# Turning the whole q, k and alpha tensors on 64x64 tiles of TensorE instead of full ones

## The chip, the cores and the metric

The kernel runs on one core of a Trainium2 chip. The metric is the device time of one execution in microseconds. The engines are called as the profile calls them: PE is TensorE (PEld its weight loads), DVE is VectorE, ACT is ScalarE, POOL is GpSimd, and SP issues DMAs.

## What is computed

A gated linear attention and behind it a gated state space block. The sizes are B = 4, H = 8, S = 768, D = 48; the second block has a model width of 384 (H times D) and 512 inner channels.

```python
for t in range(S):                                   # attention, for each of 4 x 8 heads
    state = alpha[t][:, None] * state + outer(k[t], v[t])      # 48 x 48
    y[t] = q[t] @ state
x = y, heads side by side                            # (B, S, 384)
val, gate = split(x @ w_in)                          # 512 each
h[t] = exp(A_log) * h[t-1] + val[t]                  # along the sequence
out = (silu(gate) * h) @ w_out                       # (B, S, 384)
```

## The kernel before, in words

The sequence of each batch is cut into blocks of 256 steps; there are 12 blocks, m = 0 to 11, three per batch. The function `fast` does all the work for inputs in a usual range; the function `general` is a slow way for others and does not run here. The weights come as double precision numbers and are put together from their halves by bit operations (`low` on ACT, `high` on DVE, `add_low` on POOL).

For one block the attention goes in these stages:

- q, k and alpha are loaded with the time steps along the partitions. They have to be turned, so that head and channel lie along the partitions and time along the free axis. For blocks 4 and later, and for some tensors of block 3, DVE does that (`turn`, L600). In the first blocks PE does it, by a matmul with the identity matrix or by its transpose, and ACT copies the result from PSUM to SBUF (`copy_turned`, L713 and L714).
- DVE scans alpha into running products P (`scan_P`, L635) and backwards into V (`scan_V`, L654), and multiplies: Zk = k times V (`scaled_k`, L619), Zq = q times P (`scaled_q`, L610). In blocks 0 and 2 this is done for the two chunks of 128 steps one by one.
- `scores` (PE, L798) multiplies Zq and Zk for chunk 0 and then chunk 1, `masks` (DVE L808, ACT L810) takes the lower triangle, `values`, `states` and `carried` (PE, L834, L866, L847) make the output y and the running state, `add_banks` (DVE, L894) sums the states, and `join` (L960, L963) puts the heads in their places by copies and DMAs.

The second block of the kernel follows one attention block behind: `project(n, cc)` (L988) multiplies by a quarter of `w_in`, DVE scans the value part along the sequence (L995), ACT takes the silu of the gate (L1006), and `output` or `output_parts` (L1022, L1064) multiplies by `w_out`.

Everything stands in an order written out by hand (`manual_schedule`): each engine runs its instructions in the order of the Python calls. The order at L1119 to L1228 is what matters here. The banks of PSUM that the turned tensors use are taken from a fixed list of four tags (`taken`, L682), also written by hand: a call of `bank()` takes the next one, and `bank_pair()` the next two. A bank is free again when all that read it have done so.

A raw tile of q, k or alpha holds 128 partitions by 2 times 384 values. Partition c has the steps 8c to 8c + 7 of the block, so j, from 0 to 7, is the step within a partition; i, 0 or 1, is the half of the heads. To turn a whole tensor, `turn_over` (L764) takes the j in two halves of four, each in a bank of its own, and copies each half when it is turned. `turned` (L697) has two ways. For (0, k), (1, alpha), (1, k), (1, q) and (3, alpha) it issues, for each j, one transpose of 128 columns (L702) and one of 64 columns (L703) into the same bank. For the others it issues, for each j, two matmuls (L707), one for each i, with 64 columns of the raw tile as weights and the 128 columns of the identity moving.

`turn_over` is called six times: `straighten(0, "k")` at L1124, `alphas(1)` at L1125, `alphas(2)` at L1198, `straighten(2, "k")` at L1205, `straighten(2, "q")` at L1207 and `alphas(3)` at L1220. The tensors of block 1 that are turned half by half (L1131, L1139, L1149, L1163) call `turned` directly. The very first tensors have functions of their own; `first_alphas` (L716) turns alpha of block 0 on four tiles of 64x64, with the two halves of the rows in two banks.

Of the kernel before, what the change touches and what calls it, by code (L numbers as in the profile page):

```python
# [13 lines left out]
AF = mybir.ActivationFunctionType  # L14
# [332 lines left out]
def fast(  # L347
# [22 lines left out]
    nc = tc.nc  # L370
    B, H, S, D = q.shape
# [24 lines left out]
    NJ = GC // 32  # L396
    ROW = NJ * D
# [18 lines left out]
    def steps_of(name, m):  # L416
        return raws[name][:, ds(m % 2 * (2 * ROW + 16), 2 * ROW + 16)]
# [50 lines left out]
    ident = const.tile([C, C], FP32, name="ident")  # L468
# [127 lines left out]
    def by_runs(t):  # L596
        return t.rearrange("p h (c j) -> p h c j", j=NJ)
# [89 lines left out]
    def bank(tag=None):  # L687
        if tag:
            return ps_at.tile([C, 512], FP32, tag=tag, name=tag)
        return ps_mm.tile([C, 512], FP32, tag=f"mm{next(taken)}", name="mm")  # L690

    def bank_pair(tag=None):
        return [bank(tag and f"{tag}{i}") for i in range(2)]
# [3 lines left out]
    def turned(m, name, js, t, by_transpose=None):  # L697
        raw = steps_of(name, m)
        tp = t[:, 0:len(js) * C].rearrange("p (j x) -> p j x", j=len(js))
        if (m, name) in turned_by_transpose if by_transpose is None else by_transpose:  # L700
            for n, j in enumerate(js):
                nc.tensor.transpose(tp[:, n], raw[:, ds(ROW + j * D - 64, C)], ident)  # L702
                nc.tensor.transpose(tp[0:64, n], raw[:, ds(j * D, 64)], ident)  # L703
            return tp.rearrange("p j (c h) -> p h c j", h=4)
        for n, j in enumerate(js):
            for i in range(2):
                nc.tensor.matmul(tp[ds(64 * i, 64), n], raw[:, ds(i * ROW + j * D, 64)], ident,  # L707
                                 start=True, stop=True, skip_group_check=True)
        return tp.rearrange("p j (c h) -> p h c j", h=4)

    halves = [range(0, NJ // 2), range(NJ // 2, NJ)]

    def copy_turned(to, js, tp):  # L713
        nc.scalar.activation(by_runs(to)[:, :, :, js.start:js.stop], tp, AF.Copy)  # L714
# [47 lines left out]
        return to  # L762

    def turn_over(m, name, to):  # L764
        for js in halves:
            copy_turned(to, js, turned(m, name, js, bank()))

    def alphas(m):
        turn_over(m, "a", by_place(als[m % 2])[:, :, 1:GP])

    def straighten(m, name):
        to = plain(name)
        turn_over(m, name, to)
        return to
# [171 lines left out]
    for h in range(H):  # L946
        i, e, s = h // 4, h % 4 // 2, h % 2 ^ h // 4
# [183 lines left out]
    part = turned(1, "k", halves[0], bank())  # L1131
# [7 lines left out]
    part = turned(1, "k", halves[1], bank())  # L1139
# [9 lines left out]
    part = turned(1, "q", halves[0], bank())  # L1149
# [13 lines left out]
    part = turned(1, "q", halves[1], bank(), False)  # L1163
# [27 lines left out]
    for n in range(N):  # L1191
        m = n + 1
# [223 lines left out]
```

## Time and profile before

| | |
|---|---|
| median of 3 runs | 270.44 us (270.08 to 271.02) |
| the profiled execution | 269.92 us |
| its span | 268.2 us |
| instructions in the profile | 9966 |
| TensorE clock granted | 1.0 |
| DMA | 41.19 MB in 52304 packets |

The profile's page gives for each engine the busy time and its share of the span. Its fourth part is the chain of work that ended last: from the last instruction back to what released it, step by step. The trace behind the page can be asked for single stretches: a timeline lists the instructions of an engine in order, with start, length, engine, line, operation, output and input; equal neighbours are merged, with their count behind an x, and the length then goes from the first start to the last end. An fp32 matmul stands in the trace as two records, each with a weight load, and a transpose as one. A matmul's own length holds the time through the array, so the steps from start to start tell the pace, not the lengths.

### The profile page before, as it was taken

Reading aid. Unit: us, or ns where it says so; the run is one execution under the profiler, and the core shown is the slowest. Engines: PE = TensorE matmul, PEld = TensorE weight load, DVE = VectorE, ACT = ScalarE, POOL = GpSimd, SP = SyncE. Lnnn points to the kernel's source line nnn. Section 1 sums busy time; section 2 is a strip of 40 time slices with the busy share of each in tenths; the row PEclk is TensorE's granted clock in tenths of the full one; section 3 lists DMA queues with packets and bytes.
Section 4 is the critical chain, followed back from the end, with each engine's and each line's share of the span. In section 5 each row is a group of like instructions: output and inputs, shape, how many; then the busy total and the mean of one; then the engine's idle time right before and its main releaser. Section 6 shows DMA issues by size and latency. Waiting matters only on the chain.

```text
span 268.2 us, 9966 instructions
## 1 busy us (share of the span) xinstructions
PE 263.3 (98%) x4168; PEld 230.4 (86%) x4168; DVE 233.8 (87%) x316; ACT 111.6 (42%) x270; POOL 165.9 (62%) x185
## 2 busy tenths in 40 slices
PE   8999999999999999999999999999999999999995
PEld 6898889876688988988988988988988989988874
DVE  7979998996999999799999998999999998883440
ACT  4667766372342542532533533524524515214011
POOL 8222313084169997689985995996876986646000
PEclk9999999999999999999999999999999999999999
DMA  5947984998784569496487488569598501201101
GB/s 177 315 147 242 286 192 154 238 201 194 218 204 112 127 172 218 117 230 155 108 227 167 105 215 182 124 169 212 127 214 170 143 2 31 77 0 39 69 7 59
DMA packets 52304, 41.19 MB, mean 154 GB/s; under 512 B 27392, under 2 KB 50944, under 8 KB 52256
## 3 DMA queue, kind: packets, MB, share of 16 engines
q1 hardware_dynamic: 49328, 37.34, 56.2%
q0 software_dynamic: 1536, 2.20, 3.1%
q10 hardware_dynamic: 1392, 0.99, 1.3%
q8 instruction: 34, 0.56, 0.9%
q14 instruction: 14, 0.11, 0.1%
HBM read 32.54 MB, written 4.72 MB: 139 GB/s over the span
## 4 chain that ended last, share of the span: by engine, by line
PE 91%; DVE 2%; DMA 2%; issue 1%; ACT 1%; POOL 1%; SPq 0%; DVEq 0%; POOLq 0%
PE mm L988 47%; PE mm L1064 16%; PE y L834 4%; PE y L847 4%; PE mm L1022 4%; PE s L798 4%; PE mm L798 3%; PE s L866 3%; DMA raw_q<-in_q_dram 2%; PE mm L1377 2%; PE mm L707 1%; PE mm L702 1%; PE mm L703 1%; DVE P L635 1%; POOL w_in L556 1%
## 5 line engine op out<-in xcount | busy, mean ns | idle before, releaser
L988 PE MATMUL mm<-xT,w_in 128*128 128x256 f32 x576 | 129.5, 382 | 0.1
L988 PEld LDWEIGHTS mm<-xT,w_in 128*128 128x128 f32 x576 | 107.9, 190 | 15.9 <-issue 0.3
L1006 ACT ACTIVATE sg<-mm 128x256 f32<-128x256 f32 x48 | 18.4, 383 | 88.4 <-PE mm L988 85.3
L1008 POOL TENSOR_TENSOR f_last<-sg,hh 128x256 f32<-128x256 f32 x36 | 31.2, 874 | 24.2 <-ACT sg L1006 19.6
L886 POOL TENSOR_TENSOR sum<-sum,dS 128x192 f32<-128x192 f32 x30 | 37.5, 1251 | 3.0 <-ACT dS L874 1.4
L635 DVE TENSOR_TENSOR_SCAN P<-al,lower 128x1028 f32<-128x1028 f32 x12 | 30.3, 2521 | 0.3
L995 DVE TENSOR_TENSOR_SCAN hh<-a_dec,hh,mm 128x256 f32<-128x256 f32 x32 | 23.3, 728 | 7.8 <-PE mm L988 7.5
L654 DVE TENSOR_TENSOR_SCAN V<-al,ends 128x1028 f32<-128x1028 f32 x12 | 28.7, 2391 | 0.4
L963 POOL DMA_DIRECT2D xT<-yst x44 | 22.6, 519 | 4.9 <-ACT yst L960 3.7
L556 POOL TENSOR_TENSOR w_in<-w_in,wr 128x768 int32<-128x768 int32 x4 | 7.3, 1825 | 25.4 <-DVE wr L551 16.1
L1064 PE MATMUL mm<-wide,wr 128*128 128x192 f32 x108 | 20.8, 327 | 0.0
L818 POOL TENSOR_TENSOR AK<-AK,mask 128x512 f32<-128x512 f32 x9 | 15.6, 1729 | 7.7 <-ACT AK L814 7.6
L600 DVE STREAM_TRANSPOSE k<-raw_k 128x1024 f32<-128x1024 f32 x9 | 18.5, 2053 | 0.1
L600 DVE STREAM_TRANSPOSE q<-raw_q 128x1024 f32<-128x1024 f32 x9 | 18.3, 2035 | 0.0
L1064 PEld LDWEIGHTS mm<-wide,wr 128*128 128x128 f32 x108 | 18.0, 190 | 0.0
L874 ACT ACTIVATE dS<-s 128x384 f32<-128x384 f32 (+1 forms) x18 | 7.4, 461 | 22.3 <-PE s L866 22.3
L600 DVE STREAM_TRANSPOSE al<-raw_a 128x1024 f32<-128x1024 f32 x8 | 16.4, 2048 | 0.0
L619 DVE TENSOR_TENSOR Zk<-k,V 128x1024 f32<-128x1024 f32 (+1 forms) x14 | 16.1, 1148 | 0.1
L610 DVE TENSOR_TENSOR Zq<-q,P 128x1024 f32<-128x1024 f32 (+1 forms) x14 | 15.7, 1119 | 0.0
L1064 PE MATMUL mm<-w_out,f_last 128*128 128x192 f32 x72 | 15.6, 339 | 0.0
L847 PEld LDWEIGHTS y<-Zq,sum 48*64 48x64 f32 x656 | 11.6, 134 | 3.5 <-issue 3.2
L834 PEld LDWEIGHTS y<-AK,v 64*64 64x64 f32 x352 | 12.1, 134 | 2.9 <-issue 2.9
(188 smaller groups left out, 504.5 us busy)
## 6 DMA issues: line engine op xcount, KB each, us to landing
v<-in_v_dram SPq DMA_DIRECT2D x22, 192.0 KB, 3.8
out_dram<-o_sb SPq DMA_DIRECT2D x22, 192.0 KB, 2.5
raw_k<-in_k_dram SPq DMA_DIRECT2D x18, 184.0 KB, 4.7
raw_q<-in_q_dram SPq DMA_DIRECT2D x18, 184.0 KB, 4.5
raw_k<-in_k_dram SPq DMA_DIRECT2D x18, 176.0 KB, 5.0
raw_q<-in_q_dram SPq DMA_DIRECT2D x18, 176.0 KB, 4.8
wbits<-in_moe_w_in_dram SPq DMA_DIRECT2D x8, 384.0 KB, 4.9
raw_a<-in_alpha_dram SPq DMA_DIRECT2D x16, 184.0 KB, 3.6
```

Source lines behind the costliest of these rows:

```text
L600: nc.vector.transpose(out=by_runs(to).rearrange("p h c j -> p h j c"), in_=raws[name][:, 0:4 * ROW].rearrange("p (h j d) -> p h j d", h=4, ...
L635: nc.vector.tensor_tensor_scan(out=P, data0=al[:, 0:4 * GP], data1=lower.rearrange("p h t -> p (h t)"), initial=0.0, op0=ALU.mult, op1=ALU ...
L654: nc.vector.tensor_tensor_scan(out=V[:, ::-1], data0=al[:, 1:4 * GP + 1][:, ::-1], data1=ends.rearrange("p h t -> p (h t)")[:, ::-1], init ...
L798: nc.tensor.matmul(scs[m][c][i][ds(L * h, L), ds(p * (L + D), L + D)], Zk[rows, c, p, ds(h * L, L)], Zq[rows, u, p], start=True, stop=True ...
L834: nc.tensor.matmul(ys[m][i][ds(64 * s, 64), e, ds(c * C + h * L, L)], v_sb[rows, c, 4 * i + p, :], As[i][rows, c, p, :], start=across and ...
L847: nc.tensor.matmul(ys[m][i][ds(64 * s, 64), e, ds(u * L, L)], Ss[j][rows, p, :], Zqs[m % 2][rows, u, p, D:], start=False, stop=True, skip_ ...
L886: nc.gpsimd.tensor_add(Ss[j][:, :, 0:D], Ss[j - 1][:, :, 0:D], part)
L963: engines[n % len(engines)].dma_start(out=xT[to, a], in_=st[rows, i, e])
L988: nc.tensor.matmul((pv, pg)[vg], w_ins[cc][:, kk, vg, :], xT[:, kk, :], start=(kk == 0), stop=(kk == NK - 1))
L995: nc.vector.tensor_tensor_scan(out=hh, data0=a_dec[:, cc:cc + 1].to_broadcast([C, GC]), data1=pv, initial=prev_h[cc][:, GC - 1:GC] if n % ...
L1008: f = lambda: engine.tensor_mul(fs[n][cc], sg, hh)
L1064: nc.tensor.matmul(o, a[:, k], b[k] if type(b) is list else b[:, k], start=start and k == 0, stop=k == KC - 1, skip_group_check=True)
```

## The change

`turn_over` no longer calls `turned`. It takes both banks at once, and for each j issues four matmuls on a quarter of the array each: i is the half of the heads, and with it the half of the output's partitions, and r is the half of the raw tile's partitions. Weights are 64 rows by 64 columns of the raw tile, the moving operand is the 64x64 corner of the identity that belongs to r, and the result goes to the bank of r. When all eight j are turned, two copies on ACT follow, one for each r. As r is a half of the partitions c, copy r writes 128 neighbouring steps, with all eight j; before, a copy wrote four of every eight steps. All six calls of `turn_over` go this way, the three that were transposes too.

```diff
     def turn_over(m, name, to):
-        for js in halves:
-            copy_turned(to, js, turned(m, name, js, bank()))
+        raw = steps_of(name, m)
+        parts = [t.rearrange("p (j x) -> p j x", x=64) for t in bank_pair()]
+        for j in range(NJ):
+            for i, r in ((0, 0), (1, 1), (1, 0), (0, 1)):
+                rows = ds(64 * r, 64)
+                nc.tensor.matmul(parts[r][ds(64 * i, 64), j], raw[rows, ds(i * ROW + j * D, 64)],
+                                 ident[rows, rows], start=True, stop=True, skip_group_check=True)
+        for r, part in enumerate(parts):
+            nc.scalar.activation(by_runs(to)[:, :, ds(16 * r, 16)], part.rearrange("p j (c h) -> p h c j", h=4), AF.Copy)
```

The lines behind it move down by seven in the changed kernel. The order of the instructions on the other engines, the number of banks taken and the direct calls of `turned` stay as they are.

## The prediction

> **What bounds the kernel now.** First the page: the busy shares, and the chain of work that ended last.
>
> ```profile
> PE 263.3 (98%) x4168; PEld 230.4 (86%) x4168; DVE 233.8 (87%) x316; ACT 111.6 (42%) x270; POOL 165.9 (62%) x185
> ...
> PE 91%; DVE 2%; DMA 2%; issue 1%; ACT 1%; POOL 1%; SPq 0%; DVEq 0%; POOLq 0%
> ```
>
> TensorE (PE) is nearly always busy and is 91% of the chain, so PE time that goes looks like time saved. But the change lies wholly between 8.8 and 41.5 us, so I ask that part alone, with the view of stretches (start:end, length, then each engine's busy us and count, then the granted clock):
>
> ```profile
> 8.00:13.30 5.30, 5.30 (x54) 4.93 (x50) 5.13 (x7) 3.75 (x8) 0.09 (x1) 1.00 1.04 316
> 13.30:27.20 13.90, 13.87 (x373) 12.21 (x372) 12.06 (x21) 10.08 (x24) 3.65 (x2) 1.00 0.63 200
> 27.20:44.50 17.30, 17.25 (x424) 15.35 (x424) 16.30 (x26) 11.55 (x24) 4.14 (x3) 1.00 0.81 224
> 44.50:268.00 223.50, 220.37 (x3241) 192.75 (x3234) 194.06 (x244) 83.06 (x208) 151.22 (x165) 1.00 0.59 140
> ```
>
> The third busy column is VectorE (DVE). In the first and third stretch it has 5.13 of 5.30 and 16.30 of 17.30 us: beside a full PE stands an almost full DVE. Where both are full, taking work from one gives only the little that the other has to spare. So the question is not how much PE time goes, but where PE then meets DVE.
>
> **Price of one turn.** A whole tensor is turned in 16 matmuls (two per j). On the chip an fp32 transpose is one record, an fp32 matmul two. The first row below is the matmul turn of k(2), from the PE timeline; then the first and the last of the 40 transposes that turn k(0), alpha(1) and half of k(1) without a break; then the 64x64 matmuls of `values`, their durations and their stretch (PE busy is the first number behind the comma):
>
> ```profile
> 31.73 1.97 PE L707 MATMUL mm<-ident,raw_k 128*64 128x128 f32 x32
> ...
> 8.83 0.27 PE L702 MATMUL mm<-ident,raw_k 128*128 128x128 f32 x1
> ...
> 13.09 0.27 PE L703 MATMUL mm<-ident,raw_k 128*64 128x128 f32 x1
> ...
> L834 PE MATMUL y<-AK,v x16: 217/218/218, 41.7 to 42.2; 64*64 64x64 f32 x16
> ...
> 41.70:42.40 0.70, 0.65 (x32) 0.54 (x32) 1.00 0.66 224
> ```
>
> The L707 turn: (1.97 - 0.27) / 31 = 55 ns from record to record, 32 records, 1.75 us. The transposes come to the same: 39 steps in 13.09 - 8.83 = 4.26 us are 0.109 each, and 16 of them 1.75 us. After the change a turn is 32 matmuls, 64 records, on four tiles (two row halves by two column halves), each tile with its own rows and bank or columns. L834 goes over the same four tiles: (0.65 - 0.22) / 31 = 14 ns per record, and 15 in its slower call. So 64 records take 0.88 to 0.97 us; I take 0.94. Each of the six turns loses **0.8 us** of PE, 4.9 in all. Bounds for this unrun form: L834's 14 ns below, and above two tiles at a time instead of four, which is 28 ns and the old 1.75 us.
>
> [...]
>
> Going to 64x64 tiles costs 0.09 more than a step among full ones (the scores at 13.29, below, start 0.20 behind the last transpose, not 0.11). The two activations per turn stay 512 elements each, as before, so about 0.60 us each; they now both wait for the whole turn instead of half of it.
>
> **First stretch: k(0) and alpha(1).** DVE, and then PE and ACT, from their timelines:
>
> ```profile
> 9.05 2.30 DVE L654 TENSOR_TENSOR_SCAN V<-al,ends 128x1028 f32<-128x1028 f32 x1
> ...
> 11.46 0.69 DVE L619 TENSOR_TENSOR Zk<-k,V 128x512 f32<-128x512 f32 x1
> ...
> 13.27 0.68 DVE L610 TENSOR_TENSOR Zq<-q,P 128x512 f32<-128x512 f32 x1
> 14.41 0.42 DVE L808 TENSOR_TENSOR A<-s,mask 128x256 f32<-128x256 f32 x1 [0.46 <-PE s L798]
> ...
> 15.14 0.42 DVE L808 TENSOR_TENSOR A<-mm,mask 128x256 f32<-128x256 f32 x1
> ```
>
> ```profile
> 13.29 1.00 PE L798 MATMUL s<-Zq,Zk 48*64 48x112 f32 x32
> 14.11 0.99 PE L798 MATMUL mm<-Zq,Zk 48*64 48x112 f32 x32
> ```
>
> ```profile
> 10.78 0.60 ACT L714 ACTIVATE k<-mm 128x512 f32<-128x512 f32 x1 [0.28 <-PE mm L703]
> ```
>
> Now Zk waits for the second copy of k, 10.78 + 0.60 = 11.38, a shade behind the scan V (11.35). After: the k turn runs 8.92 to about 10.1, the copies 10.1 to 11.3, and the first one holds all of chunk 0 (row half 0 is steps 0 to 127). Zk then starts behind V alone, at 11.39: 0.07 earlier. PE would be at `scores(0)` 1.4 us earlier (2 x 0.8 less two changes of tiling), but chunk 1 needs the second Zq, which ends at 13.27 + 0.68 - 0.07 = 13.88. So its scores go from 14.11 to 13.92: **0.19 of the 1.4 us arrive**. Chunk 0 is far earlier, but only ends DVE's 0.46 us of idleness ahead of its own masks; the masks of chunk 1 (15.14) still follow the scores of chunk 1.
>
> **Second stretch: alpha(2).** From those masks a line runs through ACT and DVE to POOL:
>
> ```profile
> 16.16 1.09 ACT L543 ACTIVATE wr<-wbits 128x768 uint16<-128x768 uint32 x1
> ...
> 17.59 0.33 ACT L933 ACTIVATE wide_S<-s 128x192 f32<-128x192 f32 x1
> ```
>
> ```profile
> 17.95 0.36 DVE L935 TENSOR_TENSOR wide_S<-s,wide_S 128x192 f32<-128x192 f32 x1 [1.06 <-ACT wide_S L933]
> ```
>
> ```profile
> 25.37 1.82 POOL L556 TENSOR_TENSOR w_in<-w_in,wr 128x768 int32<-128x768 int32 x1 [6.15 <-DVE wr L551]
> ```
>
> ```profile
> 25.20 1.97 PE L707 MATMUL mm<-ident,raw_a 128*64 128x128 f32 x32
> 27.25 2.86 PE L988 MATMUL mm<-xT,w_in 128*128 128x256 f32 x12
> ```
>
> ```profile
> PEld mm L988 <- POOL w_in L556: 0.3, 1, 0.3
> ```
>
> `project(0, 1)` at 27.25 waits for POOL's second block of w_in (25.37 + 1.82 = 27.19), even behind the long turn. A turn shorter by 0.8 only lengthens that wait: nothing. POOL's line (masks, ACT's wr and wide_S, DVE's sums, scans P and V, wr) moves with the masks, so PE is at 27.06, still 0.19 ahead.
>
> **Third stretch: k(2), q(2), alpha(3).** Here PE has no wait at all, and turns q behind k:
>
> ```profile
> 33.53 1.92 PE L707 MATMUL mm<-ident,raw_q 128*64 128x128 f32 x32
> 35.38 0.92 PE L988 MATMUL mm<-xT,w_in 128*128 128x256 f32 x3
> ```
>
> ```profile
> 32.64 0.33 ACT L810 ACTIVATE dS<-mm 128x192 f32<-128x192 f32 x1
> 32.87 0.60 ACT L714 ACTIVATE k<-mm 128x512 f32<-128x512 f32 x1
> ```
>
> A new wait: q's two banks were the scores' of chunk 1, and dS (32.64 + 0.33, less 0.19: 32.78) reads the second last, while PE would want it at 32.4. Behind that waiting matmul stands all of PE. The q turn then ends at 33.75, `project(0, 2)` starts at 33.9 instead of 35.38: PE is 1.5 us ahead, and 2.3 behind alpha(3), less a short wait for the state sums (39.31 + 0.4 on DVE, below). So PE would come to `scores(2)` at 41.0. But:
>
> ```profile
> 39.31 1.61 DVE L894 TENSOR_TENSOR sum<-s,sum 128x192 f32<-128x192 f32 x4
> ...
> 41.43 0.68 DVE L610 TENSOR_TENSOR Zq<-q,P 128x512 f32<-128x512 f32 x1
> ...
> 42.64 0.68 DVE L610 TENSOR_TENSOR Zq<-q,P 128x512 f32<-128x512 f32 x1
> 43.90 0.42 DVE L808 TENSOR_TENSOR A<-s,mask 128x256 f32<-128x256 f32 x1 [0.58 <-PE s L798]
> ```
>
> ```profile
> 42.90 0.95 PE L798 MATMUL s<-Zq,Zk 48*64 48x112 f32 x32
> 43.67 0.95 PE L798 MATMUL mm<-Zq,Zk 48*64 48x112 f32 x32
> 44.54 2.64 PE L988 MATMUL mm<-xT,w_in 128*128 128x256 f32 x11
> ```
>
> DVE's row of work back to the masks of `scores(1)` has no hole, and nothing of it gets shorter: it is 0.19 earlier. Its last Zq ends at 43.32 - 0.19 = 43.13, so the chunk 1 scores start at 43.17 instead of 43.67. **Sum: 0.50 us**, 0.19 inherited and 0.31 that DVE was ahead of PE. From 44.5 on PE is full to the end and the rest shifts with it; nothing there is changed. 269.92 - 0.50 = 269.4 for the profiled execution. The median of the runs shown is 270.44, 0.52 above that execution, so I forecast 270.44 - 0.50 = **269.9**.
>
> **Rivals.**
> (a) *All that PE saves in the third stretch counts*: 0.19 + 2.3 = 2.5, 267.9. It needs the second Zq by about 41.8, that is DVE 1.3 us shorter or otherwise arranged. For: PE is 91% of the chain. Against: 16.30 of 17.30 us busy, in the same order.
> (b) *Only two tiles run at once*, 28 ns a record. A turn stays 1.75 us, and changes of tiling come on top: two in the first stretch (0.09, and about as much back), so chunk 1's scores go from 14.11 to about 14.3, and the whole line is 0.2 later: 270.6. Against: the 14 ns of L834. [...]
> (c) *The clock falls: slower.* PE now stands idle from about 26.1 to 27.06 and again ahead of 41.9. The longest hole it has survived is shorter:
>
> ```profile
> 7.35 1.09 PE L750 MATMUL mm<-ident,raw_q 128*64 128x128 f32 x16 [0.51 <-DMA raw_q<-in_q_dram]
> ...
> L723 PE MATMUL s<-ident,raw_a x32: 247/311/366, 3.9 to 5.1; 64*64 64x64 f32 x32
> ...
> L723 PE MATMUL y<-ident,raw_a x32: 218/218/311, 4.8 to 5.6; 64*64 64x64 f32 x32
> ```
>
> Records of one shape go from 311 to 218 ns at about 5.1 us, some 4 us behind PE's first matmul. If a hole of 1 us at 26.1 drops the clock to half, 4 us of work at half speed lose 2 us in `project(0, 1)` and `scores(1)`, ahead of DVE's full line, so nothing hides it: 270.44 + 2 - 0.3 = 272.1. It decides between a hole of 0.5 us (clock stays 1.00) and 1 us, which no row shows. [...]
>
> **How the numbers follow.** Forecast 0.82, (a) 0.06, (b) 0.08, (c) 0.04. The forecast's own range: 0.2 to 0.6 us of gain (turns of 0.88 to 1.2 us and the small steps), and the three runs before, which spread over 270.08 to 271.02, a third of a per cent, so 269.3 to 270.6. To hold eight in ten over all cases, with (b) and some of that spread: 269.0 to 270.9. A measurement of this kernel tells 0.3%, 0.8 us, from no change. Half a microsecond is inside: same 0.67. Faster 0.24: (a), and 0.18 from the forecast where the gain is above mine or the spread helps. Slower 0.09: (c), and 0.05 from (b) and the spread.
>
> **What would show it.** Turns of 64 records in 0.9 to 1.0 us between first and last start. Zk(0) behind V at 11.4; chunk 1's scores at 13.9; a wait of about 1 us for POOL's w_in ahead of 27.06; q(2)'s first records held until 32.8; `scores(2)` held by DVE, chunk 1 at 43.2; from there every row earlier by the same 0.5; granted clock 1.00 throughout. It is wrong if a DVE operation between 28 and 43 us gets shorter or longer in its new company, if the copies read the new banks slower than 0.60, or if the shift at 44.5 isn't kept to the end.

## The result, and the profile after

The changed kernel is slower: 280.25 us median of 4 runs (275.74 to 282.81) against 270.37 us (270.08 to 271.02, 4 runs) for the kernel before; the ratio is 1.0254 (95% interval 1.0219 to 1.029). The ratio leaves out the two longest of the four runs, whose mean granted clock was 0.988 and 0.982, so it is smaller than the ratio of the two medians (1.037). The forecast was 269.9 us, with a range of 269.0 to 270.9: wrong, in sign as well.

The profiled execution took 275.74 us, 5.82 more than that of before. From its page: the busy time of PE, the clock, the DMA queue that the page calls instruction (packets, MB, share) and the engines on the chain that ended last.

```profile
PE 262.0 (96%) x4408; PEld 227.6 (83%) x4408; DVE 233.9 (85%) x316; ACT 111.0 (41%) x270; POOL 165.7 (60%) x185
...
PEclk9999999799999999999999999999999999999999
...
q8 instruction: 35, 0.57, 0.9%
...
PE 89%; issue 3%; DVE 2%; DMA 2%; ACT 1%; POOL 1%; SPq 0%; DVEq 0%; POOLq 0%
```

PE is busy for *less* time than before (262.0 against 263.3 us) in a span that is 5.8 us *longer*, with 240 more records (4408 against 4168). "issue", time in which an engine waits for nothing that the profile shows, went from 1.1% to 3.4% of the chain (the page rounds to 1% and 3%), some 6 us. One slice of the clock is down to 7 tenths. So the question is what PE stood still for. The view of stretches says where:

```profile
8.00:13.30 5.30, 3.91 (x145) 3.34 (x142) 5.13 (x7) 2.91 (x6) 0.07 (x1) 1.00 1.04 322
13.30:27.20 13.90, 13.43 (x407) 11.58 (x405) 11.63 (x20) 10.02 (x23) 3.45 (x2) 1.00 0.63 200
27.20:44.50 17.30, 14.32 (x471) 12.09 (x471) 15.89 (x24) 10.75 (x23) 3.82 (x3) 1.00 0.82 222
44.50:60.00 15.50, 13.80 (x233) 11.60 (x237) 10.59 (x21) 6.22 (x14) 3.90 (x5) 0.89 0.76 176
60.00:274.00 214.00, 210.26 (x3080) 184.09 (x3070) 184.32 (x225) 77.94 (x198) 147.65 (x161) 1.00 0.56 133
```

In the first stretch PE is idle for 1.4 us, where it was full before. In the third it is idle for 3.0 us, where it had 0.05 before; the fourth has another 1.7 us of idleness and a clock of 0.89. PE's timeline, cut to the turns and to the places where it stood (the bracket at the end of a line is the idle time before it, and what ended it):

```profile
8.78 1.16 PE L770 MATMUL mm<-ident,raw_k 64*64 64x64 f32 x64
9.76 1.09 PE L770 MATMUL mm<-ident,raw_a 64*64 64x64 f32 x59
12.24 0.34 PE L770 MATMUL mm<-ident,raw_a 64*64 64x64 f32 x5 [1.39 <-issue]
...
25.73 1.16 PE L770 MATMUL mm<-ident,raw_a 64*64 64x64 f32 x64
27.44 0.91 PE L995 MATMUL mm<-xT,w_in 128*128 128x256 f32 x3 [0.55 <-POOL w_in L556]
...
31.81 1.11 PE L770 MATMUL mm<-ident,raw_k 64*64 64x64 f32 x64
32.88 1.48 PE L770 MATMUL mm<-ident,raw_q 64*64 64x64 f32 x64
34.30 1.56 PE L995 MATMUL mm<-xT,w_in 128*128 128x256 f32 x6
...
36.56 0.27 PE L841 MATMUL y<-A,v 64*64 64x64 f32 x1 [0.43 <-issue]
...
41.63 0.73 PE L770 MATMUL mm<-ident,raw_a 64*64 64x64 f32 x33 [1.57 <-issue]
...
42.85 0.92 PE L854 MATMUL y<-Zq,sum 48*64 48x64 f32 x47
46.20 0.27 PE L854 MATMUL y<-Zq,sum 48*64 48x64 f32 x1 [2.44 <-issue]
46.33 1.00 PE L805 MATMUL s<-Zq,Zk 48*64 48x112 f32 x32
47.12 0.98 PE L805 MATMUL mm<-Zq,Zk 48*64 48x112 f32 x32
48.02 4.54 PE L995 MATMUL mm<-xT,w_in 128*128 128x256 f32 x12
...
60.89 0.58 PE L854 MATMUL y<-Zq,sum 48*64 48x64 f32 x25 [0.42 <-issue]
```

Two things are to be seen. The turns are as fast as was forecast: (1.16 - 0.22) / 63 = 15 ns a record. And PE stands in the *middle* of a group whose operands are all there: 5 and 33 records before the end of a turn (12.24, 41.63), at the last of the 48 records of `carried` (46.20). One of these is forecast (27.44, POOL's w_in); the others end with "issue", which names no releaser. The ledger against the kernel before: the first stop makes the scores of chunk 1 of block 0 0.24 us later (14.35 against 14.11). `project(0, 2)` starts at 34.30, 1.08 us earlier; three stops (36.56, 41.63, 46.20) turn this into 3.45 us later at the second scores of block 2 (47.12 against 43.67). From the start of `project(0, 3)` at 48.02 to that of `project(0, 4)` at 53.83 it takes 5.81 us instead of 4.12, since for 3.4 of them the clock is at half, as the stretch below shows; the stop at 60.89 adds 0.64. From there to the end every row is 5.8 later.

```profile
48.30:51.70 3.40, 3.40 (x9) 2.69 (x9) 3.29 (x6) 0.84 (x3) 0.10 (x1) 0.50 0.58 146
```

DVE confirms that it isn't the holder: its last Zq of block 2 is done by 43.5, about where it was before, and then it waits 3.85 us for PE.

```profile
11.29 0.69 DVE L619 TENSOR_TENSOR Zk<-k,V 128x512 f32<-128x512 f32 x1
...
42.82 0.69 DVE L610 TENSOR_TENSOR Zq<-q,P 128x512 f32<-128x512 f32 x1
47.37 0.42 DVE L815 TENSOR_TENSOR A<-s,mask 128x256 f32<-128x256 f32 x1 [3.85 <-PE s L805]
```

**Where PE stops.** Count the instructions of PE and PEld in the order of their start (a record and its weight load are two), with the semaphore instructions that the trace has for their sequencer. The five unnamed stops of the fence stand at numbers 193 + 256 times 1, 6, 7, 8 and 10; a shorter one at 20.37 is times 3. The instruction queue moved 0.57 MB in 35 packets, 16 KB each, and PE's 4408 records and as many loads are 34.4 times 256. So in these traces PE's instructions seem to come in blocks of 256, about 128 records with their loads, and PE stops where a block ends. The stretches between the entries into neighbouring blocks, first of the changed kernel and then of the kernel before:

```profile
31.95:36.55 4.60, 4.17 (x144) 3.30 (x135) 4.49 (x7) 4.23 (x10) 1.19 (x1) 1.00 1.01 217
36.55:41.63 5.08, 3.50 (x127) 2.88 (x128) 4.88 (x10) 1.45 (x4) 1.81 (x1) 1.00 0.65 162
41.63:46.20 4.57, 2.13 (x128) 1.99 (x128) 1.88 (x4) 1.80 (x3) 1.06 (x2) 1.00 0.48 173
```

```profile
32.45:37.79 5.34, 5.34 (x131) 4.73 (x131) 5.24 (x6) 4.51 (x8) 0.50 (x1) 1.00 1.03 238
37.79:42.63 4.84, 4.84 (x146) 4.38 (x139) 4.64 (x11) 2.18 (x6) 1.82 (x1) 1.00 0.51 131
42.63:47.85 5.22, 5.22 (x141) 4.48 (x136) 4.52 (x9) 3.10 (x9) 2.07 (x4) 1.00 0.46 149
```

(Records that reach over an edge are counted on both sides.) Before, a block held 4.8 to 5.3 us of work there and no stop. Now the blocks hold 2.1 to 4.2 us of work, but still take 4.6 to 5.1. The DMA view of 43.8 to 44.9 us, ahead of the longest stop's end, has the transfer: one packet of 16 KB, which the trace has from 43.84 to 44.85; no other packet of this queue starts between 39 and 47.4.

```profile
q8 instruction: 1, 0.02, 5.7%
```

PE's last record ahead of the stop ended at 43.76 and the next one began at 46.20, 1.35 us behind the end of the transfer. The other four long stops end 1.33 to 1.46 us behind the end of one.

### The profile page after: what moved, and what is told of

Read it like the earlier page. It is cut to its first block, busy times and chain, and to the rows that moved or that the text cites. A ratio compares the mean times of both kernels' runs of the same rounds, so it can differ in the third digit from the quotient of the medians.

```text
span 274.0 us, 10453 instructions
## 1 busy us (share of the span) xinstructions
PE 262.0 (96%) x4408; PEld 227.6 (83%) x4408; DVE 233.9 (85%) x316; ACT 111.0 (41%) x270; POOL 165.7 (60%) x185
## 4 chain that ended last, share of the span: by engine, by line
PE 89%; issue 3%; DVE 2%; DMA 2%; ACT 1%; POOL 1%; SPq 0%; DVEq 0%; POOLq 0%
PE mm L995 46%; PE mm L1071 16%; PE y L841 4%; PE y L854 4%; PE mm L1029 4%; PE s L805 4%; PE mm L805 3%; PE s L873 3%; PE mm L770 2%; DMA raw_q<-in_q_dram 2%; PE mm L1384 2%; DVE P L635 1%; POOL w_in L556 1%; ACT wr L543 0%; PE mm L750 0%
## 5 line engine op out<-in xcount | busy, mean ns | idle before, releaser
L995 PE MATMUL mm<-xT,w_in 128*128 128x256 f32 x576 | 131.1, 386 | 0.6 <-POOL w_in L556 0.6
L995 PEld LDWEIGHTS mm<-xT,w_in 128*128 128x128 f32 x576 | 109.1, 192 | 16.7 <-POOL w_in L556 0.7
L893 POOL TENSOR_TENSOR sum<-sum,dS 128x192 f32<-128x192 f32 x30 | 39.2, 1308 | 3.2 <-ACT dS L881 1.4
L854 PE MATMUL y<-Zq,sum 48*64 48x64 f32 x656 | 14.6, 221 | 2.9 <-issue 2.9
```

The lines of the kernel that those rows point to most:

```text
L854: nc.tensor.matmul(ys[m][i][ds(64 * s, 64), e, ds(u * L, L)], Ss[j][rows, p, :], Zqs[m % 2][rows, u, p, D:], start=False, stop=True, skip_ ...
L893: nc.gpsimd.tensor_add(Ss[j][:, :, 0:D], Ss[j - 1][:, :, 0:D], part)
L995: nc.tensor.matmul((pv, pg)[vg], w_ins[cc][:, kk, vg, :], xT[:, kk, :], start=(kk == 0), stop=(kk == NK - 1))
```

## The theories

**Theory A, supply.** The new turns issue 64 records in 0.94 us where 16 or 32 took 1.75, so a block of 256 instructions is used up before the next is there. From `scores(1)` at 30 us to `project(0, 3)` PE has 524 records where it had 412. The time then depends on how many instructions lie in a dense stretch, and on where in it the ends of the blocks fall. (Theory B of the expectations is the opposite: PE waits for data or banks, and the clock falls in such holes.)

**The rivals.** One: the new matmuls, or the operations beside them, stall by their own nature (the banks, two row halves at once, the ACT copies); stops would then stay with the same matmuls wherever the block ends fall, and go when the form goes. Two: the clock; it would have to fall ahead of the holes, not behind them. Three: the tile pace; the supply would not matter if the same matmuls were issued two tiles at a time, in the old 1.75 us.

## The experiments

All pads stand in place of a part of `keep_warm` at the very start, where PE works on zeros. A pad of small zero matmuls adds instructions there, so the ends of all blocks counted behind it move.

**The changed kernel, all block ends moved.** 48 more records ahead (26 matmuls on zeros in place of two larger ones):

```diff
-    keep_warm(3, 256)
+    keep_warm(1, 256)
+    t = bank("y0")
+    for _ in range(26):
+        nc.tensor.matmul(t[0:32, 0:16], ...)
```

> The changed kernel with 48 more TensorE records (small matmuls of zeros) ahead of the first data, where PE waits for DMA anyway. Theory A (PE runs out of instructions: they come in blocks of 16 KB, 128 matmul records each, and a block comes no faster than about one in 4.5 us): stalls stand at record numbers counted from the first one, near 221 + 127 k, so each that is left stands at a matmul 48 records earlier in the program; third stretch as slow as before, 274 to 283 us. Theory B (PE waits for data or banks, and the clock falls in such holes): the stalls stay at the same matmuls as in the changed kernel (60th of alpha(1), 32nd of alpha(3), 48th of the last carried).

Measured: 276.96 us median (276.07 to 279.68) against 270.36 on the same chip, ratio 1.0257 (1.0189 to 1.0325). The stops went to other places, all again at 193 + 256k of the new count: the turn of q(2) 28 records after its start, `states`, and, far behind the change, the last record of a `scores`:

```profile
35.91 0.80 PE L770 MATMUL mm<-ident,raw_q 64*64 64x64 f32 x36 [0.47 <-issue]
...
41.28 0.24 PE L873 MATMUL s<-v,dS 64*48 64x48 f32 x1 [1.83 <-issue]
...
172.90 0.31 PE L805 MATMUL mm<-Zq,Zk 48*64 48x112 f32 x1 [1.68 <-issue]
```

The places of 36.56, 41.63 and 46.20 in the changed kernel run here without a stop. A stop that moves with the count, and into code that the change doesn't touch, is no property of the matmul that it hits. The first rival falls. The second does too: the granted clock of the profiled execution (277.05 us) is 1.00. The pad itself cost 1.46 us at the start, so the time says little.

**Half of the records.** Only j = 0 to 3 are turned, and each copy writes them twice, so this kernel leaves half of the turning out:

```diff
-        for j in range(NJ):
+        for j in range(NJ // 2):
...
+            for n in range(2):
+                nc.scalar.activation(by_runs(to)[:, :, ds(16 * r, 16), ds(n * NJ // 2, NJ // 2)], part[:, 0:NJ // 2]...)
```

> The changed kernel, but each turn does j = 0 to 3 only and copies these to the places of j = 4 to 7 too, so half the turning is left out: 32 records per turn, on the same four tiles, with the same two banks and the copies behind them. Theory A: the stretch from 27 to 44 us needs 428 records and not 524, so there is at most a small stall; 269.3 to 271.0 us. Theory B: PE waits for DVE longer than in the changed kernel, so the holes are longer and the clock falls at least as often; 275 us or more.

Measured: 275.84 us (275.01 to 275.93), 1.0184 (1.0153 to 1.0215). Theory A's figure, as I had put it, missed, and the time is in the range of theory B: a smaller count did not take the stops away. They stand on block ends again (18.76, 23.43, 42.15, 93.73, 133.42). With fewer records all block ends fall elsewhere, and that had not been in my reckoning. The clock also fell to half for 6.8 us, behind holes of no more than 1.1 us, the longest of them a wait for DVE. Half speed for 6.8 us is, as an estimate, up to 3.4 of the 5.5 us; that part is the clock's, as theory B has it, while stops in unchanged code at 93.73 and 133.42 are not:

```profile
41.06 0.46 PE L856 MATMUL y<-Zq,sum 48*64 48x64 f32 x16 [1.10 <-DVE sum L903]
42.15 0.27 PE L843 MATMUL y<-AK,v 64*64 64x64 f32 x2 [0.40 <-issue]
```

```profile
43.30:50.30 7.00, 6.79 (x79) 5.77 (x74) 5.40 (x10) 3.04 (x8) 2.06 (x4) 0.51 0.53 145
```

**The first two turns alone** (k of block 0, alpha of block 1; the other four as before):

```diff
+        if (m, name) not in ((0, 'k'), (1, 'a')):
+            for js in halves:
+                copy_turned(to, js, turned(m, name, js, bank()))
+            return
```

> The new turn for k(0) and alpha(1) alone, all later ones as before the change. Theory A: one stall near record 221 ahead of the first scores, worth about 0.2 to 0.6 us, and none later; 270.4 to 271.2 us. Theory B: the hole ahead of the first scores alone, without a lower clock; 270.0 to 270.6 us. If the copies from the new banks were the cause, a third of the whole loss, 272 us or more.

Measured: 274.60 us (272.28 to 276.42), 1.0131 (1.0045 to 1.0217), above A's figure. It lies where slow copies were to put it, but the four copies from the new banks take 0.59 to 0.60 us each, where those of the kernel before take 0.60 (k) and 0.68 to 0.69 (alpha). Besides the stops near the new turns (11.71 and 20.96) there is one nearly 180 us behind them, where nothing is changed but the count:

```profile
190.15 0.81 PE L1075 MATMUL mm<-w_out,f_last 128*128 128x192 f32 x4 [1.55 <-issue]
```

**The last three turns alone** (k and q of block 2, alpha of block 3), by the same edit with the other list:

```diff
+        if (m, name) not in ((2, 'k'), (2, 'q'), (3, 'a')):
```

> The new turn for k(2), q(2) and alpha(3) alone. Theory A: 524 records from 27 to 44 us as in the changed kernel, at 4.5 us for 128, so 3 to 4 us lost there, and 1.7 more where a stall is long enough for the clock to fall; 273 to 279 us. Theory B: PE waits for DVE ahead of the third scores, a hole of about 1 us, no loss but for the clock; 270 to 272 us.

Measured: 281.28 us median of four (273.12, 280.99, 281.58, 281.68), above A's range as well; with one run 8 us below the other three, no ratio is given. The profiled execution has stops on block ends of 2.66 (42.48), 0.93 (45.96) and 2.64 us (194.89), and the clock at half for 6.8 us with each of the two long ones. So each part of the change can cost several us by itself; with the spread it can't be told which costs more.

These four led to a second form of theory A: not the number of instructions alone decides, but **which work lies between two block ends**. All code behind an added instruction gets new block ends, and the kernel before may simply have good ones. That asks for the next five.

**Two tiles at a time.** The same 32 matmuls a turn, in another order:

```diff
-        for j in range(NJ):
-            for i, r in ((0, 0), (1, 1), (1, 0), (0, 1)):
+        for pair in (((0, 0), (1, 1)), ((1, 0), (0, 1))):
+            for j, (i, r) in ((j, x) for j in range(NJ) for x in pair):
```

> The changed kernel with the same 32 matmuls per turn in another order: only two of the four tiles are used at a time, so a turn should take about 1.8 us, the time of the old one, instead of 0.95. Theory A (instructions come in blocks of 256, a block no faster than about one in 4.5 us; the count per stretch decides, not the pace): the stalls stay, every one on the grid of 256 instructions; 273 to 282 us. If the fast turns themselves or the holes behind them were the cause: the order of before in time, 270.0 to 270.8 us.

Measured: 279.04 us (278.26 to 282.2), 1.036 (1.0292 to 1.0427). A turn now takes as long as the old ones, (1.73 - 0.22) / 57 = 26 ns a record:

```profile
8.47 1.73 PE L770 MATMUL mm<-ident,raw_k 64*64 64x64 f32 x58
...
22.43 0.21 PE L925 MATMUL y<-A,wide 64*64 64x64 f32 x1 [1.71 <-issue]
...
193.09 1.19 PE L805 MATMUL mm<-Zq,Zk 48*64 48x112 f32 x17 [2.33 <-issue]
```

All its stops are on block ends again. The pace does count in the dense stretch, which I had denied: between 31 and 47 us 0.78 us of stops are left (46.03), where the changed kernel had 4.44. But the time is no better, for the stops stand elsewhere: 22.43, 151.38 (0.73 us) and 193.09, the last two in code that the change doesn't touch. So the third rival falls too: a slower turn doesn't take the supply out of the account. And as this kernel has as many instructions as the changed one, the blocks that end at 151.38 and 193.09 hold the same matmuls as there, where they made no stop: the place of the block ends doesn't decide alone.

**The kernel before, unchanged but for a pad of 96 records.**

```diff
-    keep_warm(3, 256)
+    keep_warm(1, 256)
+    ts, zero = [bank("y0"), bank("y1")], nc.const_aps.tensor(0.0, [C, 32], FP32)
+    for x in range(50):
+        half = ds(64 * (x % 2), 64)
+        nc.tensor.matmul(ts[x % 2][ds(64 * (x // 2 % 2), 32), 0:8], zero[half], zero[half, 0:8], ...)
```

> The kernel before the change, with all its old turns; 96 more TensorE records (48 small matmuls of zeros) ahead of the first data. Theory A: the blocks of 256 instructions now end at other places of the same program, so some of them hold only short matmuls; stalls on the grid, one of them near 190 us as in the kernel with only the first two turns new, which has the same shift; 270.6 to 276 us. Without theory A the padding lies in a wait for DMA: 270.1 to 271.2 us.

Measured: 276.86 us (273.10 to 279.18) against 270.26, 1.0196 (1.0123 to 1.0269). The trace is that of the longest run. None of the new turns is in this kernel, and it has the same illness:

```profile
18.16 0.27 PE L918 MATMUL y<-AK,wide 64*64 64x64 f32 x1 [0.71 <-issue]
...
23.14 0.21 PE L918 MATMUL y<-A,wide 64*64 64x64 f32 x1 [1.72 <-issue]
```

```profile
23.60:27.20 3.60, 3.60 (x72) 3.35 (x67) 3.00 (x4) 1.67 (x5) 0.00 (x0) 0.53 0.86 270
```

Both stops are on block ends, and so is one of 2.9 us at 194.54; the clock is at half for 3.4 us with the last two. The row at 194.54 names POOL's AK as the releaser, but its matmul doesn't read AK; a transfer of instructions had ended 1.34 us ahead of it.

**The kernel before with a pad of 128 records, one whole block.** The control: block ends fall on the same matmuls as in the kernel before. The edit is the same with `range(66)`.

> The kernel before the change with 128 more records ahead of the first data, which is one whole block, so that all later blocks are cut as before: a control for the same kernel with 96. Theory A: no stall on the grid at 18, 23 or 194 us; only what the padding takes by itself ahead of the first data, 270.3 to 271.6 us. If the padding itself were what made the other one slow: 275 us or more.

Measured: 271.56 us (270.47 to 272.73) against 270.65, 1.0046 (1.0027 to 1.0064). More instructions than the pad of 96, and a quarter of its cost. Its trace has no stop on a block end; every row of PE from 14.1 us on is 0.5 to 0.6 later, which the pad cost at the start, and the third stretch, 0.55 later, is full again:

```profile
27.75:45.05 17.30, 17.25 (x424) 15.36 (x424) 16.29 (x26) 11.56 (x24) 4.12 (x3) 1.00 0.80 225
```

96 against 128 records is the plainest evidence for theory A in this study: the same matmuls cost more or less with the place of the block ends.

**The changed kernel, padded** by 14 records, so that all block ends behind the last turn fall where they did before. The edit is that of the pad of 96, with `keep_warm(2, 256)` and `range(8)`.

> The changed kernel with 14 more records ahead of the first data, so that behind the last turn its blocks of instructions are cut at the same places as before the change (240 + 14 records are two blocks). Theory A: no stall behind 62 us; the stretch from 27 to 48 us is as slow as in the changed kernel, since it holds as many instructions; 273 to 280 us, with less spread from run to run.

Measured: 274.68 us (272.56 to 277.13), 1.0122 (1.0074 to 1.017): about half of the loss. In the dense part the stops stay; behind 60 us, where the ends are the old ones, PE is idle for 2.9 of 212 us (3.7 of 214 in the changed kernel, 3.1 of 208 before), and none of it on a block end. The profiled execution of the changed kernel had only one stop there (60.89, 0.42 us), so these two traces say little on that part; the medians do.

```profile
37.30 0.27 PE L770 MATMUL mm<-ident,raw_q 64*64 64x64 f32 x2 [2.35 <-issue]
...
45.95 0.40 PE L854 MATMUL y<-Zq,sum 48*64 48x64 f32 x12 [1.76 <-issue]
```

```profile
60.00:272.00 212.00, 209.10 (x3021) 183.01 (x3019) 186.20 (x225) 77.44 (x196) 144.71 (x160) 1.00 0.58 137
```

**The first two turns alone, padded** by 32 records: with the 96 that the two turns add, one whole block. The edits are those of the first two turns alone and of the pad, with `range(18)`.

> The new turn for k(0) and alpha(1) alone, with 32 more records ahead of the first data: 96 + 32 are one block, so from alpha(1) on the blocks are cut as before the change. Theory A: the stalls at 21 and 190 us of the same kernel without padding are gone; 270.0 to 270.9 us instead of 272 to 276. Without theory A: as without padding, 272 to 276 us.

Measured: 271.98 us (271.07 to 272.57), 1.0053 (1.0034 to 1.0073), against 274.60 without the pad; theory A's range ended at 270.9. The late stop is gone; the same `output_parts` row as in the fence of the kernel without the pad has no idle time before it:

```profile
189.38 0.76 PE L1075 MATMUL mm<-w_out,f_last 128*128 128x192 f32 x3
```

But stops of 0.18 (17.12) and 1.64 us (21.93) remain, which I had expected to go. The block that ends at 17.12 now begins within the faster turns, and PE comes to its end sooner. The block from 17.12 to 21.93 holds the same matmuls as one at 16.18 to 19.15 in the kernel before, which made no stop. There the transfer began 0.04 us after PE had entered the block and took 1.35 us; here it began 1.66 us after and took 1.76. This kernel also has no stop ahead of its first scores, so it tests the first stretch by itself (below).

**No more records than before, and only the turn of q(2) on four tiles.** k(2) and alpha(2) by transposes save 32 records, which q(2) takes:

```diff
-    turned_by_transpose = ((0, "k"), (1, "a"), (1, "k"), (1, "q"), (3, "a"))
+    turned_by_transpose = ((0, "k"), (1, "a"), (1, "k"), (1, "q"), (2, "a"), (2, "k"), (3, "a"))
...
+        if (m, name) != (2, "q"):
+            for js in halves:
+                copy_turned(to, js, turned(m, name, js, bank()))
+            return
```

> The new turn for q(2) alone (32 records more), and k(2) and alpha(2) by transposes instead of matmuls (16 records fewer each): as many TensorE records as before the change, and from q(2) on the blocks are cut at the same places. Theory A: no stall on the grid of 256 instructions, and PE gains the 0.8 us of one turn, of which 0.3 reach the end, since VectorE bounds the third scores; 269.7 to 270.6 us, ratio 0.997 to 1.001. If each fast turn cost by itself: 270.8 us or more.

Measured: 270.05 us (269.52 to 273.52) against 270.65, 0.9983 (0.9956 to 1.001): not told apart from no change, and the only version with a turn on four tiles that isn't slower. Its trace runs 0.42 later from the start. DVE and then PE at the second scores of block 2:

```profile
43.05 0.68 DVE L610 TENSOR_TENSOR Zq<-q,P 128x512 f32<-128x512 f32 x1
```

```profile
43.79 1.00 PE L809 MATMUL mm<-Zq,Zk 48*64 48x112 f32 x32
...
55.62 0.81 PE L858 MATMUL y<-Zq,sum 48*64 48x64 f32 x39 [0.33 <-issue]
```

Zq ends at 43.73 and PE starts 0.06 later: held by DVE, as the prediction had it. 43.67 + 0.42 - 43.79 = 0.30 us are gained. Then a stop at a block end (55.62), where I had expected none, costs 0.6.

## Why the prediction was wrong

**The price of a turn**: right, 0.94 us forecast and 0.94 measured, on four tiles at once; two at a time are 26 ns a record (28 were estimated in rival (b)).

**First stretch**: Zk(0) did come right behind V (11.29, V from 8.89), but that gave no 0.07: it was behind V before as well, 2.41 us after V's start then and 2.40 now. And the 0.19 at the scores of chunk 1 doesn't exist. The padded kernel with the first two turns shows it (chunk 1 at 14.61, with DVE's line 0.50 later than before): its last Zq ends at 14.46, but PE waits on until the copy of k(1) is through at 14.55 and frees the bank, and this copy waits for the second Zk. The prediction missed this wait.

```profile
14.61 1.00 PE L809 MATMUL mm<-Zq,Zk 48*64 48x112 f32 x32 [0.21 <-ACT k L714]
```

It was there before, hidden behind a full PE: ACT's timeline of the kernel before has the copy end at 14.05, and chunk 1 started at 14.11. In the changed kernel itself the first stop came on top, and chunk 1 was 0.24 later than before. The copy:

```profile
13.45 0.60 ACT L714 ACTIVATE k<-mm 128x512 f32<-128x512 f32 x1
```

**Second stretch**: right in its mechanism. The faster turn of alpha(2) (25.73) only lengthened the wait for w_in (0.55 us of idleness at 27.44, where about 1 us ahead of 27.06 was forecast), and the clock stayed at 1.00 over it.

**Third stretch**: right in its mechanism as long as PE had instructions. q(2) was held as forecast (its 64 records take 1.48 us); `project(0, 2)` came 1.27 us earlier against the start of `project(0, 1)`, where 1.29 was forecast; and DVE limits what arrives, 0.30 us in the version with q(2) alone against 0.31 forecast.

**The step that failed** is "From 44.5 on PE is full to the end and the rest shifts with it; nothing there is changed", and ahead of it "PE would come to `scores(2)` at 41.0": it came at 46.33. Both rest on the price of a turn, which counted PE time and no instructions. The six turns add 240 records, 480 instructions with their loads. They make the blocks between 31.95 and 46.20 too short for the supply (36.56 to 46.20: 4.5 us lost against the 1.08 that PE was ahead), and they move every block end behind them. By these rows the change without any stop would be worth an estimated 0.3 us, the third stretch alone; no run had all six turns and no stop.

**Rivals.** None was this one. The clock did fall, as in (c), but not behind the hole at 26.1 that (c) named: it fell after the stop of 2.44 us at 46.20, for 3.4 us at half, and cost 1.7 of the 5.8 us. In other runs it fell after shorter holes, down to 1.1 us, but not after every one (1.64, 1.83 and 2.35 us, last section).

**What stays open**: when a transfer starts. For the stops of the changed kernel it began 1.1 to 2.4 us, and for the last one 5.0, after PE entered the block before. But blocks of 2.3 to 2.4 us at 150, 190 and 228 us in the changed kernel made no stop: there the transfer had begun 0.4 to 4.2 us before PE entered the block; and in the kernel before one of 2.97 us at 16 went well with a transfer that began 0.04 us behind, and blocks of 2.28 and 2.14 us at 144 and 184 with transfers that began 2.3 and 3.0 us ahead. So in these two traces a short block was a risk and no certain stop; those of 2.1 to 3.0 us without one had a transfer that had begun by 0.04 us after PE entered them. What the transfers wait for wasn't tried. Nor is it shown what the 1.33 to 1.46 us from its end to PE's next record are. The spread of the versions with stops (275.7 to 282.8 for the changed kernel) fits chance in these starts and in the clock, but that is only argued.

## What to carry to other kernels

Count instructions as well as time: an fp32 matmul cost PE four of them here (the 32 of a new turn are 64 records and 64 loads in the trace), and where PE ran dry between 32 and 46 us a block of 128 records came every 4.6 to 5.1 us, 36 to 40 ns a record, whether it held 4.2 or 2.1 us of work. Before a matmul is cut into smaller ones, look at how much PE time lies in each run of 128 records. And when unchanged code gets slower in the middle of a group, with "issue" as the releaser, count instructions to it: if the place is a multiple of 256 from the other stops, as here, pad the kernel by a part and by the whole of a block (here 96 and 128 records, ratios 1.0196 and 1.0046) before blaming the code.

## What the runs showed that I had not expected

- 96 records on zeros at the start of an otherwise unchanged kernel made it longer by a ratio of 1.0196, and 128 by 1.0046.
- Blocks of the same matmuls made a stop in one kernel and not in another: two with two tiles at a time, at 151.38 and 193.09, made none in the changed kernel.
- The clock fell to half for 3.4 or 6.8 us with holes in PE's work of 1.1 (half of the records), 1.72 (pad of 96), 2.33 (two tiles), 2.44 (the changed kernel), 2.66 (last three turns) and 2.9 us (pad of 96); it did not after 1.64 (first two turns, padded), 1.83 (moved block ends) and 2.35 us (changed kernel, padded). So in these runs no length of hole decides alone.
- The records of the 64x64 turns started 15 ns apart on four tiles in turn (the changed kernel), and 26 ns apart with two tiles at a time.
